# A second group entered plainly, audits pinned in order, and transposes ahead of scores, in a fused gated-attention and MLP kernel

## The chip, the cores and the metric

One core of one Trainium2 chip. The time is the device time of one execution in microseconds, the median of three runs. PE is the tensor engine, DVE VectorE, ACT ScalarE, POOL GpSimd, SP the engine that issues all transfers here.

## The reference

Recurrent gated linear attention (4 sequences, 8 heads, 768 tokens, head size 48), whose output, 3072 tokens by 384, goes through an MLP with SiLU:

```python
for t in range(S):
    state = alpha[:, :, t, :, None] * state + einsum('bhd,bhe->bhde', k[:, :, t], v[:, :, t])
    y[:, :, t] = einsum('bhd,bhde->bhe', q[:, :, t], state)
x = y.transpose(0, 2, 1, 3).reshape(3072, 384)
h = x @ w_in                       # 384 x 2048
out = (h / (1 + exp(-h))) @ w_out  # 2048 x 384
```

The kernel takes float32 q, k, v, alpha and 64-bit weights, which it turns into float32 itself.

## The kernel before

**Chunks.** The tokens are cut into 24 chunks of 128 (6 places in a sequence, 4 sequences; chunk n has place n // 4, so chunks 0 to 3 begin their sequences). A chunk n goes through four stages: `products` transposes a, k and q on PE (line 620), copies the decay out with ACT (622) and runs two scans and two products on DVE (625 to 636), which give `u`, `p`; `scores` multiplies them (647), masks the scores on DVE (651) and transposes k back (655); `values` makes the output (680), which ACT puts into `xt`; `states` updates the recurrent state (693, 699). Each step of the main loop emits scores(n-1), products(n), values(n-1), states(n-1) in this order, with a slot of other work behind each stage.

**The MLP.** Four chunks make a group, six groups in all. `enter` multiplies a group by w_in with a fast block scheme of 20 block products (`PRODUCTS`) instead of 24; it needs sums of blocks of x (`sums_x`, 11 on DVE) and of w_in (`sums_w`, 23 on DVE, some in place), and DVE puts the products together (770) before SiLU (767). `enter_plain` is the ordinary product (737), with SiLU straight from PSUM (740). `leave` is the output by w_out: plain for the first half of group 0 (884), a fast scheme of 7 steps (857) otherwise, which needs `differences` of blocks of w_out (540 to 542, 897) and sums of its own input (`side_by_side`, 845; 862). A matmul of float32 has two records in the profile. Before, group 0 is entered plainly and groups 1 to 5 by the scheme.

**Weights and audit.** SP loads 12 blocks of w_in and 16 of w_out as bit pairs (461); ACT and DVE turn each into float32 (564, 567 to 569). Later `audit` reads alpha (9 transfers), w_in (12) and w_out (16) once more, 37 transfers into one buffer, and DVE reduces each to its extremes (602): 65 reduces. A flag made of them selects at the end whether a general version has to run; it doesn't here.

**Order.** Calls are emitted in the order of the main loop; `fill` runs as many `pieces` (generators of `enter`, `leave` and the rest) in a slot as a due count allows. A scheduler then orders each engine's queue by its own estimates, except that instructions handed to `keep_in_program_order` keep the order in which they were emitted. Each engine runs its queue strictly in order. PSUM's eight banks are three for the attention (`ps_a`), three for w_in (`ps_m`) and two for the output (`ps_o`).

Of the kernel before, what the change touches and what calls it, by code (L numbers as in the profile page):

```python
# [355 lines left out]
def quotients(  # L356
# [19 lines left out]
    nc = tc.nc  # L376
# [37 lines left out]

    def ps_attn(n=C):
        return ps_a.tile([128, 512], F32, name="ps_a").rearrange("p (j c) -> p j c", c=n)

# [56 lines left out]
    ident = consts.tile([128, 128], F32, name="ident")  # L474
    make_identity(nc, ident)

# [44 lines left out]
    def combine(to, sa, a, sb, b):  # L521
        if sa == sb == 1:
            dve.tensor_tensor(to, a, b, ALU.add)
        elif sa == 1:
            dve.tensor_tensor(to, a, b, ALU.subtract)
        elif sb == 1:
            dve.tensor_tensor(to, b, a, ALU.subtract)
        else:
            dve.scalar_tensor_tensor(to, a, -1.0, b, ALU.mult, ALU.subtract)

    def sums_w(upto):
        while sums_done[0] < min(upto, len(SUMS_W)):
            to, sa, a, sb, b = SUMS_W[sums_done[0]]
            combine(block_w(to), sa, block_w(a), sb, block_w(b))
            sums_done[0] += 1

    sums_done = [0]

    def differences(i):
        dve.tensor_tensor(t1[:, i], b12[:, i], b11[:, i], ALU.subtract)  # L540
        dve.tensor_tensor(t2[:, i], b22[:, i], t1[:, i], ALU.subtract)
        dve.tensor_tensor(t4[:, i], b21[:, i], t2[:, i], ALU.subtract)
# [33 lines left out]
    def audit():  # L576
# [13 lines left out]
        for src, n, kind in todo:  # L590
# [4 lines left out]
            else:  # L595
                nc.sync.dma_start(t[:, 0:n, :].rearrange("p n w -> p (n w)"), src.bitcast(I32))
                x = t[:, 0:n, 1]
            i = at[kind]
            at[kind] += 1
            for which, op in ((0, ALU.max), (1, ALU.min)):  # L600
                if kind == 1 or which == 0:
                    dve.tensor_reduce(seen[kind][which][:, i : i + 1], x, axis=AX, op=op,  # L602
                                      apply_absolute_value=True)
            yield
# [7 lines left out]
    def products(n):  # L612
# [4 lines left out]
        for name in ("a", "k", "q"):  # L617
            ps[name] = ps_attn()
# [108 lines left out]
    def enter_plain(grp, h):  # L727

        if h == 0:
            for pair in range(NQ // 2):  # L730
                g_tiles(grp, pair)
        xt = xts[2 * grp + h]
        for f in range(0, NFT, 2):
# [6 lines left out]
            act.activation(gts[grp, h, q // 2][:, i : i + 2, q % 2, :], ps, AF.Silu)  # L740
# [106 lines left out]
    def out_bank(i, n):  # L847
        return outs[i].tile([128, 512], F32, name="ps_o")[:, 0:n]

    def leave(grp, h):  # L850
# [24 lines left out]
        if grp == h == 0:  # L875
# [3 lines left out]
            for j in range(HF // 2):  # L879
# [16 lines left out]
            for i in range(0, HF, 2):  # L896
                dve.tensor_tensor(b12[:, i : i + 2], b22[:, i : i + 2], b12[:, i : i + 2], ALU.subtract)
# [6 lines left out]
        def done():  # L904
            if grp == 0:
                sums_w(12 + 2 * next(steps) + 2)
# [53 lines left out]
    def both(grp):  # L960
        last = GB * grp + GB
        pieces.append((sums_x(grp), last))
        for h in range(2):
            x, y = leave(grp - 1, h), enter(grp, h)
            for _ in range(7):
                pieces.extend(((x, last), (y, last)))
# [149 lines left out]
```

## Time and profile before

| | us |
|---|---|
| median of 3 runs | 618.42 (618.08 to 619.08) |
| profiled execution, time | 622.89 |
| profiled execution, span | 621.1 |
| PE busy | 585.3 |
| DVE busy | 435.0 |
| ACT busy | 184.7 |
| POOL busy | 5.2 |

The span is the time from the first to the last instruction in the profile; the time has what lies around it as well. The busy times overlap, and an engine that is idle while another sets the pace costs nothing. An x at the end of a row is a number of instructions; in brackets stands how long an engine was idle and what ended it.

### The profile page before, as it was taken

What the parts mean: (1) busy time and instruction counts of PE and PEld (TensorE: products, weight loads), DVE (VectorE), ACT (ScalarE), POOL (GpSimd) and SP (SyncE); (2) the same over time, 40 slices, a digit from 0 to 9 for tenths busy, and PEclk for the clock granted to TensorE, in tenths of its full rate; (3) what the DMA queues carried; (4) which work ended last, traced back from release to release, by engine and by line L of the source; (5) the groups of instructions that cost most, each with busy time, mean ns of one, the idle gap of its engine ahead of it and who ended that gap; (6) DMA issues with size and microseconds to landing.
All of it is one profiled execution on the core that took longest, in us unless ns stands there. A gap on an engine that the chain in (4) does not pass through costs nothing.

```text
span 621.1 us, 10850 instructions
## 1 busy us (share of the span) xinstructions
PE 585.3 (94%) x4450; PEld 521.4 (84%) x4450; DVE 435.0 (70%) x802; ACT 184.7 (30%) x311; POOL 5.2 (1%) x22
## 2 busy tenths in 40 slices
PE   4889989998999979999999999999999999999996
PEld 3668876697777869989978999999999999999996
DVE  3897999868978798677689577479377365444531
ACT  1335441010335434134233224224233233242200
POOL 3000000000000000000000000000000000000000
PEclk9789999997999989999998999999999999999999
DMA  9986964165664524445353233033010000000000
GB/s 208 222 173 199 249 145 86 33 152 155 171 154 85 141 59 92 137 105 115 103 133 72 71 58 52 20 55 55 20 34 1 14 14 6 20 7 13 15 20 30
DMA packets 116169, 54.25 MB, mean 87 GB/s; under 512 B 101648, under 2 KB 107792, under 8 KB 116112
## 3 DMA queue, kind: packets, MB, share of 16 engines
q1 hardware_dynamic: 116112, 53.49, 37.7%
q8 instruction: 36, 0.59, 0.4%
q14 instruction: 21, 0.17, 0.1%
HBM read 48.76 MB, written 4.72 MB: 86 GB/s over the span
## 4 chain that ended last, share of the span: by engine, by line
PE 56%; DVE 27%; DMA 12%; issue 2%; ACT 1%; POOL 1%; DVEq 0%; ACTq 0%; SPq 0%; POOLq 0%
PE ps_o L857 27%; PE ps_m L756 19%; DMA bits<-in_moe_w_out_dram 5%; DMA bits<-in_moe_w_in_dram 5%; DVE seen L602 5%; PE ps_a L680 3%; PE ps_a L620 3%; DVE g L770 3%; DVE p L634 2%; DVE u L625 2%; DMA bits<-in_alpha_dram 2%; PE ps_a L647 2%; DVE u L629 1%; DVE p L636 1%; PE ps_a L655 1%
## 5 line engine op out<-in xcount | busy, mean ns | idle before, releaser
L857 PE MATMUL ps_o<-w_out,g 128*128 128x192 f32 x704 | 126.8, 335 | 0.6 <-DVE o L871 0.6
L857 PEld LDWEIGHTS ps_o<-w_out,g 128*128 128x128 f32 x704 | 118.9, 196 | 3.8 <-issue 1.4
L857 PE MATMUL ps_o<-wt,g 128*128 128x192 f32 x528 | 91.8, 327 | 0.0
L756 PE MATMUL ps_m<-xc,w_in 128*128 128x256 f32 x360 | 88.1, 380 | 1.0 <-DVE g L770 0.9
L857 PEld LDWEIGHTS ps_o<-wt,g 128*128 128x128 f32 x528 | 86.3, 190 | 1.5 <-issue 0.8
L756 PEld LDWEIGHTS ps_m<-xc,w_in 128*128 128x128 f32 x360 | 66.9, 190 | 9.6 <-DVE g L770 1.5
L602 DVE TENSOR_REDUCE seen<-bits 128x1 f32<-128x384 int32 (+2 forms) x65 | 43.2, 689 | 36.9 <-DMA bits<-in_moe_w_out_dram 16.1
L762 ACT COPY g<-ps_m 128x512 f32<-128x512 f32 x80 | 46.8, 588 | 70.2 <-PE ps_m L756 70.2
L767 ACT ACTIVATE g<-g 128x1024 f32<-128x1024 f32 x40 | 41.2, 1054 | 74.1 <-DVE g L770 74.1
L756 PE MATMUL ps_m<-xc,wx 128*128 128x256 f32 x240 | 62.2, 381 | 0.0
L862 DVE TENSOR_TENSOR g<-g 128x512 f32<-128x512 f32 x66 | 45.1, 687 | 17.0 <-PE ps_o L857 16.9
L770 DVE TENSOR_TENSOR g<-ps_m,g 128x512 f32<-128x512 f32 x70 | 46.9, 684 | 6.9 <-PE ps_m L756 5.7
L756 PEld LDWEIGHTS ps_m<-xc,wx 128*128 128x128 f32 x240 | 43.6, 190 | 5.1 <-issue 1.0
L737 PE MATMUL ps_m<-xt,w_in 128*128 128x256 f32 x192 | 45.5, 391 | 0.5 <-DVE w_in L569 0.5
L647 PE MATMUL ps_a<-p,u 48*128 48x128 f32 x384 | 30.2, 297 | 12.5 <-DVE p L636 11.8
L647 PEld LDWEIGHTS ps_a<-p,u 48*128 48x128 f32 x384 | 25.4, 198 | 19.5 <-issue 14.0
L737 PEld LDWEIGHTS ps_m<-xt,w_in 128*128 128x128 f32 x192 | 36.4, 196 | 6.2 <-DVE w_in L569 1.0
L651 DVE TENSOR_TENSOR g<-ps_a,mask 128x512 f32<-128x512 f32 x48 | 31.6, 686 | 11.6 <-PE ps_a L647 11.2
L762 ACT COPY part<-ps_m 128x512 f32<-128x512 f32 x40 | 23.5, 587 | 52.8 <-PE ps_m L756 34.6
L625 DVE TENSOR_TENSOR_SCAN u<-al,one 128x516 f32<-128x516 f32 x24 | 29.5, 1229 | 10.9 <-ACT al L622 10.8
L770 DVE TENSOR_TENSOR g<-g,part 128x512 f32<-128x512 f32 x30 | 20.5, 683 | 17.8 <-ACT part L762 12.8
L756 PE MATMUL ps_m<-xt,w_in 128*128 128x256 f32 x120 | 31.0, 381 | 0.7 <-DVE g L770 0.7
(102 smaller groups left out, 658.4 us busy)
## 6 DMA issues: line engine op xcount, KB each, us to landing
bits<-in_moe_w_in_dram SPq DMA_DIRECT2D x24, 512.0 KB, 3.8
bits<-in_moe_w_out_dram SPq DMA_DIRECT2D x32, 384.0 KB, 3.5
an<-in_alpha_dram SPq DMA_DIRECT2D x24, 192.0 KB, 4.0
kn<-in_k_dram SPq DMA_DIRECT2D x24, 192.0 KB, 4.7
qn<-in_q_dram SPq DMA_DIRECT2D x24, 192.0 KB, 4.7
vn<-in_v_dram SPq DMA_DIRECT2D x24, 192.0 KB, 3.7
bits<-in_alpha_dram SPq DMA_DIRECT2D x9, 512.0 KB, 3.9
out_dram<-o SPq DMA_DIRECT2D x48, 96.0 KB, 1.6
```

The source lines that it names most:

```text
L602: dve.tensor_reduce(seen[kind][which][:, i : i + 1], x, axis=AX, op=op, apply_absolute_value=True)
L620: pe.transpose(ps[name][:, j, :], c[name][:, 2 * j : 2 * j + 2, :], ident)
L625: dve.tensor_tensor_scan(u[:, end - 1 :: -1], sg[:, end:0:-1], one[:, end:0:-1], 0.0, ALU.mult, ALU.add)
L647: pe.matmul(ps[u][:, j, :], lhsT=c["kp"][r, j, :], rhs=c["qp"][r, j, :], start=True, stop=True)
L651: dve.tensor_tensor(g[:, u], ps[u], mask[:, None, :].to_broadcast([128, NP, C]), ALU.mult)
L737: pe.matmul(ps[:, e, :], lhsT=w_in[:, t, (f + e) * 128 : (f + e + 1) * 128], rhs=xt[:, t, :], start=(t == 0), stop=(t == NKT - 1))
L756: pe.matmul(ps[:, e], lhsT=block_w(w)[:, 2 * pair + e], rhs=block_x(grp, x), start=(first and e == 0), stop=(e == 1), skip_group_check=True)
L762: act.copy(to, ps)
L767: act.activation(x, x, AF.Silu)
L770: dve.tensor_tensor(to, a, b, op)
L857: pe.matmul(ps, lhsT=x, rhs=w[:, i], start=(first and i == 0), stop=(i == HF - 1), skip_group_check=True)
L862: dve.tensor_tensor(cells(grp, h, pair, *to), cells(grp, h, pair, *x), cells(grp, h, pair, *y), ALU.subtract)
```

## The change

1. Group 1 is entered plainly as group 0 is. `enter_plain` now takes half of a group's w_in columns at a time (`pair`); `leave(0, 1)` stands beside group 1's second half instead of ahead of group 1; the differences of w_out go into group 1's first pieces, and the sums of w_in are made by halves, in `leave(0, 1)` and `leave(1, 0)`. `sums_x(1)` and `enter(1, ...)` no longer exist.
2. An audit's reduces are emitted one call behind its transfer and keep the order of emission; audits begin with group 2's pieces.
3. In the first four steps products(n) is emitted ahead of scores(n-1), and the transposes of k and q of the first four chunks go to the two output banks.
4. A SiLU of one column at the start loads ACT's table; the identity is made earlier.
5. `fill` counts matmuls instead of pieces, and the two empty steps behind chunk 3 are gone.

```diff
+    def out_bank(i, n):
+        return outs[i].tile([128, 512], F32, name="ps_o")[:, 0:n]
...
+    table = fix.tile([128, 1], F32, name="table")
+    dve.memset(table, 0.0)
+    act.activation(table, table, AF.Silu)
+    ident = consts.tile([128, 128], F32, name="ident")
+    make_identity(nc, ident)
...
+    def sums_w(pair, upto):
+
+        r = slice(2 * pair, 2 * pair + 2)
+        while sums_done[pair] < min(upto, len(SUMS_W)):
+            to, sa, a, sb, b = SUMS_W[sums_done[pair]]
+            tc.keep_in_program_order(
+                combine(block_w(to)[:, r], sa, block_w(a)[:, r], sb, block_w(b)[:, r]))
+            sums_done[pair] += 1
+
+    sums_done = [0] * (NQ // 2)
+
+    def differences(i):
+
+        if i < HF // 2:
+            i = slice(2 * i, 2 * i + 2)
+            tc.keep_in_program_order(
+                dve.tensor_tensor(t1[:, i], b12[:, i], b11[:, i], ALU.subtract))
+            dve.tensor_tensor(t2[:, i], b22[:, i], t1[:, i], ALU.subtract)
+            dve.tensor_tensor(t4[:, i], b21[:, i], t2[:, i], ALU.subtract)
         else:
+            i -= HF // 2
+            if i % 2 == 0:
+                side_by_side(0, 1, i // 2)
+            i = slice(2 * i, 2 * i + 2)
+            dve.tensor_tensor(b12[:, i], b22[:, i], b12[:, i], ALU.subtract)
...
             else:
                 nc.sync.dma_start(t[:, 0:n, :].rearrange("p n w -> p (n w)"), src.bitcast(I32))
                 x = t[:, 0:n, 1]
+            yield
             i = at[kind]
             at[kind] += 1
             for which, op in ((0, ALU.max), (1, ALU.min)):
                 if kind == 1 or which == 0:
-                    dve.tensor_reduce(seen[kind][which][:, i : i + 1], x, axis=AX, op=op,
-                                      apply_absolute_value=True)
-            yield
+                    tc.keep_in_program_order(
+                        dve.tensor_reduce(seen[kind][which][:, i : i + 1], x, axis=AX, op=op,
+                                          apply_absolute_value=True))
...
-            ps[name] = ps_attn()
+            if n < GB and name != "a":
+
+                ps[name] = out_bank("kq".index(name), 512).rearrange("p (j c) -> p j c", c=C)
+            else:
+                ps[name] = ps_attn()
             for j in range(NP):
                 pe.transpose(ps[name][:, j, :], c[name][:, 2 * j : 2 * j + 2, :], ident)
...
-    def enter_plain(grp, h):
+    def enter_plain(grp, h, pair):
         if h == 0:
-            for pair in range(NQ // 2):
-                g_tiles(grp, pair)
+            g_tiles(grp, pair)
         xt = xts[2 * grp + h]
-        for f in range(0, NFT, 2):
+        for f in range(8 * pair, 8 * pair + 8, 2):
             ps = bank(f // 2 % 3).rearrange("p (e n) -> p e n", e=2)
             for e in range(2):
                 for t in range(NKT):
                     pe.matmul(ps[:, e, :], lhsT=w_in[:, t, (f + e) * 128 : (f + e + 1) * 128],
                               rhs=xt[:, t, :], start=(t == 0), stop=(t == NKT - 1))
             q, i = divmod(f, 4)
-            act.activation(gts[grp, h, q // 2][:, i : i + 2, q % 2, :], ps, AF.Silu)
+            act.activation(gts[grp, h, pair][:, i : i + 2, q % 2, :], ps, AF.Silu)
+            if grp == 1 and pair == 0:
+                differences(4 * h + f // 2)
+            if grp > 0 and f % 8 == 6:
+                side_by_side(grp, h, pair)
             yield
...
-                differences(slice(2 * j, 2 * j + 2))
-                if j % 2 == 1:
-                    side_by_side(0, 1, j // 2)
-                sums_w(3 * j + 3)
                 if j < HF // 2 - 1:
                     yield
...
         def done():
-            if grp == 0:
-                sums_w(12 + 2 * next(steps) + 2)
+            if 2 * grp + h in (1, 2):
+                sums_w(2 * grp + h - 1, 4 * next(steps) + 4)
...
+    def plain(grp, h, pair):
+        return (enter_plain(grp, h, pair), 12, 2 * (2 * grp + h) + 2)
+
+    def group(grp):
+        return [[(enter(grp, pair), 12, GB * grp + GB)] * 7 for pair in range(2)]
+
+    def output(grp):
+        return [[(leave(grp, h), 12, GB * grp + GB)] * 7 for h in range(2)]
+
+    def both(x, y):
+        for i in range(max(len(x), len(y))):
+            pieces.extend(x[i : i + 1] + y[i : i + 1])
     pieces = []
-    for part, n, last in ((enter_plain(0, 0), HF, 2), (enter_plain(0, 1), HF, 4),
-                          (leave(0, 0), HF // 2, 4), (leave(0, 1), 7, 4),
-                          (sums_x(1), 1, 2 * GB), (enter(1, 0), 7, 2 * GB), (enter(1, 1), 7, 2 * GB)):
-        pieces += [(part, last)] * n
-    ALONE = 15
-    START = len(pieces) - ALONE
+    for h in range(2):
+        for pair in range(2):
+            pieces += [plain(0, h, pair)] * 4
+    pieces += [(leave(0, 0), 24, GB)] * (HF // 2)
+    phases = [len(pieces)]
+    for h in range(2):
+        pieces += [plain(1, h, 0)] * 4
+    both([(leave(0, 1), 12, GB)] * 7, [plain(1, 0, 1)] * 4 + [plain(1, 1, 1)] * 4)
+    phases.append(len(pieces))
+    before = output(1)
     for grp in range(2, NG):
-        both(grp)
-    for h in range(2):
-        pieces += [(leave(NG - 1, h), NT)] * 7
+        pieces.append((sums_x(grp), 0, GB * grp + GB))
+        for x, y in zip(before, group(grp)):
+            both(x, y)
+        phases.append(len(pieces))
+        before = output(grp)
+    pieces += before[0] + before[1]
+    work_at = [0]
+    for _, n, _ in pieces:
+        work_at.append(work_at[-1] + n)
...
-    begin = [n if n < GB else n + 2 for n in range(NT)]
-    STEPS = begin[-1] + 2
-    FIRST = 4
+    STEPS = NT + 1
     SLOTS = 4
-    STEADY = (begin[2 * GB - 1] + 1) * SLOTS + 3
+    marks = [2 * SLOTS + 2] + [(GB * i + 2 * GB) * SLOTS + 2 for i in range(len(phases))]
...
-        if step < FIRST:
+        at = step * SLOTS + slot
+        if at < marks[0]:
             if step >= 1:
-                convert(0, ((step - 1) * SLOTS + slot + 1) * 6 // ((FIRST - 1) * SLOTS))
+                convert(0, (at - SLOTS) * 3 // (marks[0] - SLOTS) + 1)
             return
-        at = step * SLOTS + slot + 1
-        if at <= STEADY:
-            share = START * (at - FIRST * SLOTS) // (STEADY - FIRST * SLOTS)
-        elif at <= STEADY + GB * SLOTS:
-            share = START + ALONE * (at - STEADY) // (GB * SLOTS)
-        else:
-            share = START + ALONE + 29 * (at - STEADY - GB * SLOTS) // (GB * SLOTS)
-            if at % 2:
-                next(audits, None)
-        while done < share and pieces[done][1] <= bridged:
+        i = next(i for i, m in enumerate(marks[1:]) if at < m)
+        a, b = [work_at[n] for n in ([0] + phases)[i : i + 2]]
+        due = a + (b - a) * (at - marks[i] + 1) / (marks[i + 1] - marks[i])
+        if i >= 2 and at % 2:
+            next(audits, None)
+        while work_at[done + 1] <= due and pieces[done][2] <= bridged:
             convert(0, 3 * (done // 2) + 6)
-            convert(1, 2 * done - 8)
+            convert(1, 3 * (done - 6) // 2)
...
     for step in range(STEPS):
-        for slot, (stage, lag) in enumerate(
-                ((scores, 1), (products, 0), (values, 1), (states, 1))):
-            if step - lag in begin:
-                n = begin.index(step - lag)
+        stages = ((scores, 1), (products, 0), (values, 1), (states, 1))
+        if step < GB:
+
+            stages = stages[1::-1] + stages[2:]
+        for slot, (stage, lag) in enumerate(stages):
+            n = step - lag
+            if 0 <= n < NT:
                 stage(n)
                 if stage is values:
                     bridged = n + 1
```

How it moves instructions. PE's queue at the start; `an`, `kn`, `qn` are the inputs alpha, k and q (the numbers tell the two buffers apart), L620 and L644 the transposes, L647 and L671 the scores. Before:

```order
L620 MATMUL ps_a<-ident,an_107 128x128 x4
L620 MATMUL ps_a<-ident,kn_111 128x128 x4
L620 MATMUL ps_a<-ident,qn_109 128x128 x4
L647 MATMUL ps_a<-p,u 128x128 x8
L655 MATMUL ps_a<-ident,u 128x128 x4
L620 MATMUL ps_a<-ident,an_108 128x128 x4
L620 MATMUL ps_a<-ident,kn_112 128x128 x4
L620 MATMUL ps_a<-ident,qn_110 128x128 x4
```

PE's queue at the start, now:

```order
L644 MATMUL ps_a<-ident,an_115 128x128 x4
L644 MATMUL ps_o<-ident,kn_119 128x128 x4
L644 MATMUL ps_o<-ident,qn_117 128x128 x4
L644 MATMUL ps_a<-ident,an_116 128x128 x4
L644 MATMUL ps_o<-ident,kn_120 128x128 x4
L644 MATMUL ps_o<-ident,qn_118 128x128 x4
L671 MATMUL ps_a<-p,u 128x128 x8
L679 MATMUL ps_a<-ident,u 128x128 x4
```

Chunk 1's transposes moved ahead of chunk 0's scores, and k and q into the output banks.

PE's queue where group 1 is entered. Before, by the scheme (L756), behind all of leave(0, 1):

```order
L647 MATMUL ps_a<-p,u 128x128 x8
L655 MATMUL ps_a<-ident,u 128x128 x4
L756 MATMUL ps_m<-xc,w_in 128x256
L620 MATMUL ps_a<-ident,an_108 128x128 x4
L620 MATMUL ps_a<-ident,kn_112 128x128 x4
L620 MATMUL ps_a<-ident,qn_110 128x128 x4
L756 MATMUL ps_m<-xc,w_in 128x256 x3
L756 MATMUL ps_m<-xc,wx 128x256 x2
```

Now, plainly (L760), with leave(0, 1) (L881) in between:

```order
L671 MATMUL ps_a<-p,u 128x128 x8
L679 MATMUL ps_a<-ident,u 128x128 x4
L881 MATMUL ps_o<-w_out,g 128x192 x8
L760 MATMUL ps_m<-xt,w_in 128x256 x6
L644 MATMUL ps_a<-ident,an_115 128x128 x4
L644 MATMUL ps_a<-ident,kn_119 128x128 x4
L644 MATMUL ps_a<-ident,qn_117 128x128 x4
L881 MATMUL ps_o<-wt,g 128x192 x8
```

The products need no `xc` and no DVE combination any more, and the output steps moved in between them.

DVE's queue where the audits begin (L602, L623); L651 and L675 mask scores. Before, ahead of group 1's products:

```order
L523 TENSOR_TENSOR xc<-xt 128x256 x2
L602 TENSOR_REDUCE seen_1918<-bits 128x1
L897 TENSOR_TENSOR w_out<-w_out 128x2x192
L699 TENSOR_TENSOR st_162<-ps_a,st_162 48x4x48 x2
L602 TENSOR_REDUCE seen_1918<-bits 128x1
L897 TENSOR_TENSOR w_out<-w_out 128x2x192
L651 TENSOR_TENSOR g<-ps_a,mask 128x512 x2
L602 TENSOR_REDUCE seen_1918<-bits 128x1
```

Now, beside group 2's products (L797 puts these together, L886 is `subtract` in `leave`):

```order
L723 TENSOR_TENSOR st_165<-ps_a,st_165 48x4x48 x2
L623 TENSOR_REDUCE seen_1873<-bits 128x1
L797 TENSOR_TENSOR g<-g,part 128x512
L886 TENSOR_TENSOR g<-g 128x2x2x128 x2
L675 TENSOR_TENSOR g<-ps_a,mask 128x512 x2
L797 TENSOR_TENSOR g<-g,part 128x512
L886 TENSOR_TENSOR g<-g 128x2x2x128 x2
```

The reduces moved back by more than a group and stand between the pieces of the scheme.

More of the change, by code (lines that the diff above doesn't have):

```diff
@@ L522, in combine @@
         if sa == sb == 1:
[L523 to L527, printed above, removed]
-        else:
[L529 to L542, printed above, removed]
+            return dve.tensor_tensor(to, a, b, ALU.add)
+        if sa == 1:
+            return dve.tensor_tensor(to, a, b, ALU.subtract)
+        if sb == 1:
+            return dve.tensor_tensor(to, b, a, ALU.subtract)
+        return dve.scalar_tensor_tensor(to, a, -1.0, b, ALU.mult, ALU.subtract)
+    def sums_w(pair, upto):
[13 more added lines that the diff above has]
+            dve.tensor_tensor(t4[:, i], b21[:, i], t2[:, i], ALU.subtract)
+        else:
+            i -= HF // 2
[3 more added lines that the diff above has]
+            dve.tensor_tensor(b12[:, i], b22[:, i], b12[:, i], ALU.subtract)
     def weights(which):
@@ L845, in side_by_side @@
         dve.tensor_tensor(x, x, cells(grp, h, pair, 1, 1), ALU.add)
-    def out_bank(i, n):
-        return outs[i].tile([128, 512], F32, name="ps_o")[:, 0:n]
     def leave(grp, h):
@@ L895, in leave @@
                     store(m, c, ps[m][:, c * HO : (c + 1) * HO])
-            for i in range(0, HF, 2):
-                dve.tensor_tensor(b12[:, i : i + 2], b22[:, i : i + 2], b12[:, i : i + 2], ALU.subtract)
             yield
```

9 lines of the change are left out of this document (removed).

## Prediction

> **What bounds the kernel now.** I read the head of the page first, then the busy time of each engine in four stretches, then the chain of waits where the tensor engine (PE) never stops, then the start of the timeline. The head says that PE is nearly always occupied:
>
> ```profile
> span 621.1 us, 10850 instructions
> PE 585.3 (94%) x4450; PEld 521.4 (84%) x4450; DVE 435.0 (70%) x802; ACT 184.7 (30%) x311; POOL 5.2 (1%) x22
> ```
>
> Busy matmuls are not matmuls at full pace, so I price PE by start-to-start times where nothing holds it up. The chain of waits from 330 us on (start, us, what) gives them:
>
> ```profile
> 333.36 1.31 PE ps_a L620 x12
> 334.67 2.60 PE ps_o L857 x16
> 337.28 2.59 PE ps_m L756 x12
> 339.87 1.67 PE ps_a L680 x56
> 341.54 2.80 PE ps_o L857 x16
> 346.92 0.88 PE ps_a L693 x8
> 353.01 1.09 PE ps_a L647 x16
> 354.10 0.58 PE ps_a L655 x4
> ```
>
> So a w_in record (256 columns) costs 2.59/12 = 0.216 us, a w_out record 0.1625, and of a chunk the transposes (T) 1.31, scores with their transpose (S) 1.67, values (V) 1.87 (the matmuls behind it start 0.2 late: 2.80 against 2.60) and states (St) 0.88. An L884 piece of 16 records goes start to start in 103.50 - 98.33 = 5.17:
>
> ```profile
> 98.33 5.33 PE L884 MATMUL ps_o<-w_out,g 128*128 128x384 f32 x16
> 103.50 0.60 PE L620 MATMUL ps_a<-ident,an 128*128 128x128 f32 x4
> ```
>
> The stretches are cut where group 0's plain matmuls run freely (51.8), at the end of L884 (123.1) and where output begins beside group 2's w_in work (227.0):
>
> ```profile
> 0.00:51.80 51.80, 37.66 (x324) 29.77 (x325) 36.27 (x65) 16.13 (x26) 5.16 (x22) 0.90 0.99 193
> 51.80:123.10 71.30, 68.19 (x426) 52.38 (x425) 68.51 (x135) 21.59 (x41) 0.00 (x0) 1.00 0.56 141
> 123.10:227.00 103.90, 93.62 (x869) 81.59 (x869) 83.86 (x144) 32.44 (x55) 0.00 (x0) 0.97 0.58 141
> 227.00:621.10 394.10, 385.83 (x2836) 357.65 (x2834) 246.41 (x460) 114.55 (x190) 0.00 (x0) 0.99 0.22 50
> ```
>
> At full pace their work is: first, 4 chunks of 4.96 (V is 1.1 in a sequence's first chunk, which has no state part) and 324 - 4 x 72 = 36 plain records, 27.6; second, 156 plain records 33.7, L884 20.8, T4 to T6, S4, S5, V4, V5, St4, St5 12.8, together 67.3; third, one leave 112 x 0.1625 = 18.2, enter(1) 160 x 0.216 = 34.6, S6 to S12, T7 to T12, V6 to V11, St6 to St11 36.1, together 88.9; fourth, four enters 138, ten leaves 182, the other chunk work 60, together 380.2. All in all 564.0. Lost are therefore 24.2 + 4.0 + 15.0 + 13.9 = 57.1 us, and 5.5 of the last 13.9 lie behind the last matmul. The change can only win from these losses; PE's work it raises.
>
> In the third stretch DVE causes the loss. Line 602 is the audit's reduce. DVE takes its instructions in order, so when a reduce waits for its own transfer, all of DVE's work behind it waits too: 36.9 us in all, and it is in this stretch that PE waits for DVE:
>
> ```profile
> L602 DVE TENSOR_REDUCE seen<-bits 128x1 f32<-128x384 int32 (+2 forms) x65 | 43.2, 689 | 36.9 <-DMA bits<-in_moe_w_out_dram 16.1 <-DMA bits<-in_moe_w_in_dram 13.1 <-DMA bits<-in_alpha_dram 7.7
> 136.89 2.78 PE L857 MATMUL ps_o<-wt,g 128*128 128x192 f32 x16
> 141.91 2.08 PE L647 MATMUL ps_a<-p,u 48*128 48x128 f32 x16 [2.24 <-DVE p L636]
> 145.75 4.21 PE L857 MATMUL ps_o<-w_out,g 128*128 128x192 f32 x16
> ```
>
> After the wait of 2.24 us the same scores take 2.08 instead of 1.09 and the same 16 records 4.2 instead of 2.77: a wait is paid twice, since the granted clock falls to half.
>
> **The change part by part.**
>
> *Group 1 plainly.* 192 records in place of 160: 32 x 0.216 = +6.9 us on PE, all on the path. In return sums_x(1) and enter(1)'s DVE combinations are gone from the third stretch, and leave(0,1) goes there from before. PE's third stretch is then plain(1) 41.5, leave(0,1) 18.2, four chunks 22.9. For DVE I estimate four chunks at 6.6 (two scans, four products, the state's pieces about 1.4), 16 differences at 0.5, leave(0,1) with about ten operations at 0.6, side by side 5 x 0.6, half of the w_in sums 23 x 0.42: some 53 us beside 82 of PE. Before, DVE was busy 83.86 of 103.9 there, audits among it.
>
> ```profile
> L625 DVE TENSOR_TENSOR_SCAN u<-al,one 128x516 f32<-128x516 f32 x24 | 29.5, 1229 | 10.9 <-ACT al L622 10.8
> L651 DVE TENSOR_TENSOR g<-ps_a,mask 128x512 f32<-128x512 f32 x48 | 31.6, 686 | 11.6 <-PE ps_a L647 11.2
> ```
>
>  I expect 3 us lost instead of 15.0; ends 0 and 9 (half the drop kept by other waits).
>
> *Sums by pair.* 46 instructions of 256 columns for 23 of 512, 46 x 0.418 - 23 x 0.682 = +3.5 us of DVE, off the path: half stands beside leave(0,1), half beside leave(1,0), where DVE has a quarter of the time free.
>
> ```profile
> L523 DVE TENSOR_TENSOR xc<-xt 128x256 f32<-128x256 f32 x15 | 6.1, 418 | 0.1
> L523 DVE TENSOR_TENSOR w_in<-wx,w_in 128x512 f32<-128x512 f32 x4 | 2.6, 682 | 0.0
> ```
>
> *Audit in order.* The reduces come a slot or more behind their transfers and begin only with group 2, so all 43.2 us of DVE go to the fourth stretch, where it is busy 246 of 394 (some 20 of the 43 were there before). SP's audit transfer still waits for the reduce that frees the one buffer, and the next chunk's v load and the output stores stand behind it. By DVE's new order the two audits of a chunk come some 2 to 4 us apart, a transfer lands 3.8 us after its issue, so I expect DVE to wait a microsecond or two at some of them. That such a wait reaches PE the trace denies: between 280 and 320 DVE waited up to 2.24 us for audit transfers, and PE was full.
>
> ```profile
> 280.00:300.00 20.00, 20.00 (x163) 18.52 (x163) 14.31 (x26) 7.00 (x13) 0.00 (x0) 1.00 0.55 121
> 300.00:320.00 20.00, 19.95 (x171) 17.87 (x169) 14.97 (x31) 3.84 (x6) 0.00 (x0) 1.00 0.50 123
> 320.00:340.00 20.00, 17.85 (x111) 16.09 (x113) 19.04 (x40) 8.18 (x14) 0.00 (x0) 0.91 0.40 84
> bits<-in_moe_w_in_dram SPq DMA_DIRECT2D x24, 512.0 KB, 3.8
> 299.75 1.01 DVE L602 TENSOR_REDUCE seen<-bits 128x1 f32<-128x384 int32 x2 [2.24 <-DMA bits<-in_moe_w_out_dram]
> ```
>
> The loss at 320 to 340 is sums_x crowding DVE (19.04 of 20) as a group begins; it may come again at three group starts instead of two. I keep 13 lost in the fourth stretch, ends 10 and 20.
>
> *Table at once, transposes ahead.* The first decay copy waits 1.28 us for ScalarE's table; the second load, at 38.75, goes too, hidden.
>
> ```profile
> 5.38 1.28 ACT L622 ACT_TABLE_LOAD   x1 [5.38 <-PE ps_a L620]
> 6.67 0.59 ACT L622 COPY al<-ps_a 128x512 f32<-128x512 f32 x1
> 12.03 2.08 PE L647 MATMUL ps_a<-p,u 48*128 48x128 f32 x16 [4.37 <-DVE p L636]
> 21.29 1.16 PE L647 MATMUL ps_a<-p,u 48*128 48x128 f32 x16 [1.47 <-DVE p L636]
> 31.44 1.16 PE L647 MATMUL ps_a<-p,u 48*128 48x128 f32 x16
> 41.17 1.16 PE L647 MATMUL ps_a<-p,u 48*128 48x128 f32 x16 [1.00 <-DVE p L636]
> 14.73 1.09 SPq L436 DMA_DIRECT2D qn<-in_q_dram  x1
> 12.00:18.00 6.00, 5.91 (x64) 4.89 (x64) 2.60 (x4) 1.75 (x3) 0.00 (x0) 1.00 1.39 212
> 57.88 0.69 DVE L569 CUSTOM_DVE_ANT_0 w_in<-w_in,up 128x1024 uint16<-128x1024 uint16 x1
> 59.77 0.69 DVE L569 CUSTOM_DVE_ANT_0 w_in<-w_in,up 128x1024 uint16<-128x1024 uint16 x1
> ```
>
> The Trainium skill, page "ScalarE: Activation LUTs", section "What ACT_TABLE_LOAD costs", adds a drain of about 1.38 us to a load of 1.28 when the set is switched. Here the copy starts 0.01 us behind the load, so the measured 1.28 stands; by the page's 2.66 the sum would be 1.4 us lower at most.
>
> I walk the new order with these durations. Chunk 0's scan starts 1.3 earlier, but DVE now has chunk 1's scan ahead of p0, and PE has chunk 1's q transposes ahead of scores 0: those come at about 12.7, no gain. Chunk 1's p is ready near 15, not 21.1. Its scores, however, stand behind chunk 2's transposes in PE's order, and the transfers are the bound there (DMA share 1.39): q of chunk 2, issued at 14.73, lands near 19.9 (an estimate, five behind its issue), so scores 1 come at 20.5. p2 is ready at 26, but eight matmuls that need the third converted w_in block (28.7) stand ahead: scores 2 at 33, against 31.44. p3 is ready at 35.5, against 41.0. From there DVE converts without a pause (59.77 - 57.88 = 1.89 us a block): the twelfth block is done at 52.5, against 59.77 + 0.69 = 60.5. PE follows with 20 records: half of group 0 is entered at 56.8. By then 39.9 us of full-pace work is done (96 records, T0 to T4, S0 to S3, V0 to V2, St0 to St2), so 16.9 are lost instead of 24.2. Ends: 13 (table and transposes both pay in full) and 24 (nothing gained). I take 17, the walk. Behind it DVE has lost some 20 us of differences and sums, and PE does not wait in my walk up to L884: 2 lost instead of 4.0, ends 0 and 5.
>
> *Out banks for k and q.* Only chunks 0 to 3 use them; the first output product comes after, so nothing is held up. The ident and DVE memset moves cost nothing: PE's first transpose waits for a's transfer until 4.2 either way.
>
> **Sum.** 564.0 + 6.9 = 570.9 of work and 17 + 2 + 3 + 13 = 35 lost give a span of 605.9, 15.2 less than 621.1. The profiled execution took 622.89, the median of the runs is 618.42; I subtract from the latter: 603.
>
> **Rivals.**
> 1. *The start does not gain* (603 + 7 = 610): transfers are at 1.39 of their share, and chunk loads now go ahead of the weight blocks in SP's queue, so conversions wait for them. For it: three blocks land some 8 us later than before. Against: DVE has the next chunks to do meanwhile.
> 2. *PE never waits before group 2*, and the group starts are calm: 13 + 0 + 0 + 10 lost, 12 less than mine: 591; half of it 597.
> 3. *Slower: audits stall PE.* Pinned in DVE's order over the whole second half, the transfers make DVE wait for the same 36.9 us in all, and there every DVE wait has PE's bank drains right behind it. If PE feels it all, 603 + 37 = 640. It decides from 15.2/36.9 = 41% felt on. For it: the second half has no other slack than DVE's. Against it the two full rows from 280 to 320.
> 4. *A cold clock through the start*: PE works in short bursts between transfers until 35 us, at half clock, and the eight matmuls ahead of scores 2 take 7 instead of 3.5. DVE then waits some 2 to 3 us more: 606. For it, the clock of 0.57 between 24 and 30:
>
> ```profile
> 24.00:30.00 6.00, 5.78 (x52) 4.74 (x53) 5.47 (x9) 2.27 (x5) 0.00 (x0) 0.57 1.13 259
> ```
>
> The Trainium skill, "TensorE: Matmul & The Clock Gate", section "Part 1: The HAM clock gate (the "warmup" mystery)", has the clock halved after an idle window of about 3.4 us. The trace agrees in kind but is stricter: a gap of 2.24 us was enough at 141.91.
>
> **How the numbers follow.** Forecast 0.45 (its own range 599 to 607), rival 1 0.17, rival 2 0.16, rival 4 0.12, rival 3 0.07, and 0.03 that the parts cancel within 0.2% (1.2 us, about what this measurement tells from nothing). Faster 0.90, same 0.03, slower 0.07. From 594 to 612 all but about 0.2 are held: rival 3, the cancelling, and half of rival 2.
>
> **What would show it.** One table load, near 1 us; chunk 1's scores near 20.5; the last w_in conversion near 53; L884 (now L908) over near 124 with V7 behind it; leave(1,0) starting near 210 and no "seen" before about 200; full PE rows from there on but for the group starts. Wrong would be: conversions ending at 60; PE waits for DVE g or p behind L623 rows; plain(1) waiting for its Silu.

## The result and the profile after

The changed kernel takes 601.23 us (600.96 to 601.28, four runs) against 618.75 for the kernel before in the same set: a ratio of 0.9716, 95% interval 0.9699 to 0.9733, 17.5 us faster. A second set on another chip gave 601.21 against 620.85, 0.9676 (0.9655 to 0.9698). 603.0 was forecast, within 594 to 612.

The head of the page after the change (the profiled execution took 600.96 us), and the busy time of each engine in the four stretches of the prediction, cut at the same places of the program: half of group 0 entered, the last product of L908 done with chunk 7's values behind it, leave(1,0) begins.

```profile
span 599.2 us, 10853 instructions
PE 584.1 (97%) x4482; PEld 521.1 (87%) x4482; DVE 420.8 (70%) x787; ACT 171.1 (29%) x295; POOL 5.2 (1%) x22
0.00:59.94 59.94, 51.20 (x356) 39.63 (x356) 47.06 (x85) 20.04 (x34) 5.16 (x22) 1.00 1.01 214
59.94:125.34 65.40, 65.40 (x578) 50.53 (x577) 51.23 (x100) 19.91 (x40) 0.00 (x0) 1.00 0.59 136
125.34:207.99 82.65, 82.65 (x693) 74.15 (x689) 49.06 (x98) 17.01 (x32) 0.00 (x0) 1.00 0.26 47
207.99:599.20 391.21, 384.81 (x2866) 356.78 (x2862) 273.42 (x507) 114.14 (x190) 0.00 (x0) 1.00 0.29 73
```

In the second and third stretch PE's busy time equals the length of the stretch, and the granted clock is 1.00 throughout. With the prediction's unit prices the work in the four is 39.9, 65.5, 82.6 and 382.5 us, so the lost time is 20.0, 0, 0 and 8.7: 28.7 in place of the 57.1 of before and of the 35 forecast.

The start, in rows of the timeline (start, duration, engine, line, operation, idle time ahead of it): the first scan, the scores of chunks 0 to 2, the last conversion of w_in, and the matmuls with which half of group 0 is entered.

```profile
6.02 1.23 DVE L649 TENSOR_TENSOR_SCAN u<-al,one 128x516 f32<-128x516 f32 x1 [4.64 <-ACT al L646]
12.54 2.08 PE L671 MATMUL ps_a<-p,u 48*128 48x128 f32 x16
21.89 1.16 PE L671 MATMUL ps_a<-p,u 48*128 48x128 f32 x16
34.08 0.71 PE L671 MATMUL ps_a<-p,u 48*128 48x128 f32 x8
55.12 0.69 DVE L588 CUSTOM_DVE_ANT_0 w_in<-w_in,up 128x1024 uint16<-128x1024 uint16 x1
55.49 4.53 PE L760 MATMUL ps_m<-xt,w_in 128*128 128x256 f32 x20
```

Scores 0 come at 12.54 (forecast 12.7), scores 1 at 21.89 (20.5), scores 2 at 34.08 (33), the conversions end at 55.81 (52.5), group 0 is half entered at 59.94 (56.8).

The audits' reduces, by the view of their tile (count, shortest/median/longest ns, from when to when) and by the group of their line (busy, mean ns, idle time ahead of it):

```profile
L623 DVE TENSOR_REDUCE seen<-bits x65: 541/672/1221, 230.9 to 555.9; 128x1 f32<-128x384 int32 x32, 128x1 f32<-128x512 int32 x24, 128x1 f32<-128x1024 f32 x9
L623 DVE TENSOR_REDUCE seen<-bits 128x1 f32<-128x384 int32 (+2 forms) x65 | 42.5, 688 | 3.5 <-DMA bits<-in_moe_w_out_dram 1.8 <-DMA bits<-in_moe_w_in_dram 1.4
```

DVE waits 3.5 us for them in place of 36.9. That nearly all of this wait goes was not forecast: the prediction expected "a microsecond or two at some of them". Which part of the change moved it, and what it was worth, is what the experiments ask.

### The profile page after: what moved, and what is told of

The parts are those of the page before. It is cut to its first block, busy times and chain, and to the rows that moved or that the text cites. A ratio compares the mean times of both kernels' runs of the same rounds, so it can differ in the third digit from the quotient of the medians.

```text
span 599.2 us, 10853 instructions
## 1 busy us (share of the span) xinstructions
PE 584.1 (97%) x4482; PEld 521.1 (87%) x4482; DVE 420.8 (70%) x787; ACT 171.1 (29%) x295; POOL 5.2 (1%) x22
## 4 chain that ended last, share of the span: by engine, by line
PE 90%; DVE 6%; issue 1%; ACT 1%; POOL 1%; DVEq 0%; ACTq 0%; POOLq 0%
PE ps_o L881 32%; PE ps_m L783 22%; PE ps_m L760 12%; PE ps_a L704 6%; PE ps_a L644 4%; PE ps_a L671 4%; PE ps_o L908 3%; PE ps_a L717 3%; PE ps_a L679 2%; DVE g L797 1%; DVE u L649 1%; DVE w_in L588 1%; DVE u L653 1%; DVE w_in L587 1%; DVE p L658 0%
## 5 line engine op out<-in xcount | busy, mean ns | idle before, releaser
L881 PE MATMUL ps_o<-w_out,g 128*128 128x192 f32 x704 | 123.2, 328 | 0.8 <-ACT g L794 0.8
L881 PEld LDWEIGHTS ps_o<-w_out,g 128*128 128x128 f32 x704 | 114.8, 190 | 4.1 <-ACT g L794 1.4
L881 PE MATMUL ps_o<-wt,g 128*128 128x192 f32 x528 | 91.4, 326 | 0.0
L760 PE MATMUL ps_m<-xt,w_in 128*128 128x256 f32 x384 | 89.5, 382 | 1.2 <-DVE w_in L588 1.1
L881 PEld LDWEIGHTS ps_o<-wt,g 128*128 128x128 f32 x528 | 86.9, 190 | 1.0
L760 PEld LDWEIGHTS ps_m<-xt,w_in 128*128 128x128 f32 x384 | 70.4, 190 | 11.5 <-DVE w_in L588 2.2
L783 PE MATMUL ps_m<-xc,w_in 128*128 128x256 f32 x288 | 70.1, 379 | 0.0
L783 PEld LDWEIGHTS ps_m<-xc,w_in 128*128 128x128 f32 x288 | 53.5, 190 | 6.2
L886 DVE TENSOR_TENSOR g<-g 128x512 f32<-128x512 f32 x66 | 45.2, 688 | 15.7 <-PE ps_o L881 15.6
L789 ACT COPY g<-ps_m 128x512 f32<-128x512 f32 x64 | 37.5, 586 | 50.2 <-PE ps_m L783 50.2
L783 PE MATMUL ps_m<-xc,wx 128*128 128x256 f32 x192 | 50.1, 383 | 0.0
L623 DVE TENSOR_REDUCE seen<-bits 128x1 f32<-128x384 int32 (+2 forms) x65 | 42.5, 688 | 3.5 <-DMA bits<-in_moe_w_out_dram 1.8
L797 DVE TENSOR_TENSOR g<-ps_m,g 128x512 f32<-128x512 f32 x56 | 37.2, 682 | 6.2 <-PE ps_m L783 5.7
L675 DVE TENSOR_TENSOR g<-ps_a,mask 128x512 f32<-128x512 f32 x48 | 31.2, 684 | 12.3 <-PE ps_a L671 12.1
L783 PEld LDWEIGHTS ps_m<-xc,wx 128*128 128x128 f32 x192 | 35.0, 190 | 4.7 <-issue 1.2
L763 ACT ACTIVATE g<-ps_m 128x512 f32<-128x512 f32 x32 | 19.1, 597 | 62.8 <-PE ps_m L760 62.8
L797 DVE TENSOR_TENSOR g<-g,part 128x512 f32<-128x512 f32 x24 | 16.6, 690 | 24.5 <-ACT g L789 15.1
L671 PEld LDWEIGHTS ps_a<-p,u 48*128 48x128 f32 x384 | 24.6, 193 | 8.4 <-issue 7.9
L658 DVE TENSOR_TENSOR_SCAN p<-al,inv 128x516 f32<-128x516 f32 x24 | 29.5, 1230 | 0.6
```

The costliest lines, as they stand in the source:

```text
L671: pe.matmul(ps[u][:, j, :], lhsT=c["kp"][r, j, :], rhs=c["qp"][r, j, :], start=True, stop=True)
L675: dve.tensor_tensor(g[:, u], ps[u], mask[:, None, :].to_broadcast([128, NP, C]), ALU.mult)
L760: pe.matmul(ps[:, e, :], lhsT=w_in[:, t, (f + e) * 128 : (f + e + 1) * 128], rhs=xt[:, t, :], start=(t == 0), stop=(t == NKT - 1))
L783: pe.matmul(ps[:, e], lhsT=block_w(w)[:, 2 * pair + e], rhs=block_x(grp, x), start=(first and e == 0), stop=(e == 1), skip_group_check=True)
L789: act.copy(to, ps)
L797: dve.tensor_tensor(to, a, b, op)
```

## The experiments

All medians are of five to twelve runs. The kernel before took 620.5 to 621.1 us beside them.

### The audits' order, alone and taken away

The kernel before with only this edit (before_audit):

```diff
+            yield
             i = at[kind]
...
-                    dve.tensor_reduce(seen[kind][which][:, i : i + 1], x, axis=AX, op=op,
-                                      apply_absolute_value=True)
-            yield
+                    tc.keep_in_program_order(
+                        dve.tensor_reduce(seen[kind][which][:, i : i + 1], x, axis=AX, op=op,
+                                          apply_absolute_value=True))
```

> The kernel before with the audits in order as its only change. Theory A (the audits' order is most of the gain; letting them loose cost the changed kernel 13 us of span): 618.7 - 13 = 606, the third stretch loses 2 to 4 us in place of 15.0, the start is as before. Rival B (order and start work together, the steps with no chunk and the old start hold the rest): half of it, 612. Rival C (with the scheme for group 1, DVE has no room for audits in order either): 616 to 619.

601.55 us (600.73 to 604.05), 0.9682 (0.9660 to 0.9704): 19.3 us faster, as much as the whole change. All three expectations allowed too little. The tile's rows of before and of this kernel, and the group of its line:

```profile
L602 DVE TENSOR_REDUCE seen<-bits x65: 535/662/1221, 120.0 to 349.5; 128x1 f32<-128x384 int32 x32, 128x1 f32<-128x512 int32 x24, 128x1 f32<-128x1024 f32 x9
L604 DVE TENSOR_REDUCE seen<-bits x65: 541/672/1221, 228.9 to 557.1; 128x1 f32<-128x384 int32 x32, 128x1 f32<-128x512 int32 x24, 128x1 f32<-128x1024 f32 x9
L604 DVE TENSOR_REDUCE seen<-bits 128x1 f32<-128x384 int32 (+2 forms) x65 | 42.6, 688 | 24.7 <-DMA bits<-in_moe_w_out_dram 11.6 <-DMA bits<-in_moe_w_in_dram 8.4 <-DMA bits<-in_alpha_dram 4.7
```

Free to move, the reduces stood in DVE's order from 120.0 us on, some 110 us ahead of where they begin when they keep to the program's order. What one of them does to PE, in two rows of DVE's timeline of before: the reduce waits for its transfer until 137.01, the last step of p comes behind it at 141.08, and the scores at 141.91, which the prediction shows, wait 2.24 us for that p.

```profile
137.01 1.22 DVE L602 TENSOR_REDUCE seen<-bits 128x1 f32<-128x1024 f32 x1 [2.30 <-DMA bits<-in_alpha_dram]
141.08 0.68 DVE L636 TENSOR_TENSOR p<-ps_a,p 128x512 f32<-128x512 f32 x1
```

In the third stretch of before (123.1 to 227.0) DVE was busy for 83.9 us, some 20 of them with reduces, waited 17.2 us for audits and 2.4 us for other things: 103.5 of 103.9 us, so it had no time to spare. Cut at the same places of the program, the third and fourth stretch of before_audit are:

```profile
124.03:214.82 90.79, 89.19 (x870) 79.50 (x869) 66.51 (x118) 32.46 (x55) 0.00 (x0) 1.00 0.34 60
214.82:602.30 387.48, 381.80 (x2836) 354.42 (x2834) 265.71 (x487) 114.49 (x190) 0.00 (x0) 1.00 0.30 74
```

PE's work is the same as in before, 88.9 and 380.2 us by the prediction, so the third stretch loses 1.9 us in place of 15.0 and the fourth 7.3 in place of 13.9. DVE still waits 24.7 us for audits, all in the fourth stretch, where it is busy for only 265.7 of 387.5 us, and PE hardly notices. PE's longest waits behind 125 us, by what they waited for (total, times, longest), in before and then in this kernel (its list ends with the second row):

```profile
PE ps_a L655 <- DVE st L699: 4.6, 4, 2.2
PE ps_m L756 <- DVE g L770: 4.0, 3, 2.3
PE ps_a L647 <- DVE p L636: 3.3, 2, 2.2
```

```profile
PE ps_a L656 <- DVE st L700: 1.4, 3, 0.7
PE ps_a L648 <- DVE p L637: 0.5, 1, 0.5
```

The whole lists add up to 12.9 and 1.9 us. The rest is the clock, the last column but two: behind 125 us three stretches of before fall below full clock, two of which are shown, and the same places of this kernel do not.

```profile
140.00:160.00 20.00, 17.21 (x158) 16.43 (x160) 16.93 (x30) 1.65 (x3) 0.00 (x0) 0.83 0.58 155
220.00:240.00 20.00, 17.53 (x103) 16.05 (x103) 19.57 (x41) 7.37 (x12) 0.00 (x0) 0.91 0.28 57
```

```profile
140.00:160.00 20.00, 19.59 (x193) 17.63 (x191) 15.24 (x32) 4.00 (x7) 0.00 (x0) 1.00 0.39 73
320.00:340.00 20.00, 20.00 (x176) 18.32 (x175) 11.48 (x21) 5.56 (x11) 0.00 (x0) 1.00 0.26 71
```

(0.17 + 0.09 + 0.09) x 20 = 7.0 us of full-clock time, with 320 to 340 us at 0.91 as the prediction shows it. 11.0 of waits and 7.0 of clock make 18.0, beside 18.8 between the two spans (621.1 and 602.3). PE's busy time says much the same: for the same 4450 records it falls by 8.1 us from the 585.3 of before, so 10.7 of the 18.8 were idle time.

```profile
PE 577.2 (96%) x4450; PEld 516.0 (86%) x4450; DVE 436.3 (72%) x802; ACT 184.4 (31%) x311; POOL 5.1 (1%) x22
```

The reverse, the changed kernel with the reduces emitted as before (audit_loose):

> The changed kernel with the audits' reduces emitted as before, free to be moved ahead in DVE's order. Theory A: they move ahead of their transfers into the third stretch again, DVE waits for audit transfers about 35 us in place of 3.5, a part reaches PE at the products of chunks 6 to 12: 601.2 + 5 to 10 = 606 to 611. Rival B (the plan with plain group 1 gives DVE the room): DVE's waits come back but PE does not feel them, 601 to 603.

615.29 us (613.89 to 617.18), 14.1 more than the changed kernel: theory A, and more than it allowed. The reduces run from 112.3 to 330.7 us, DVE waits 46.7 us for them, and PE loses in two stretches that are full, or nearly, in the changed kernel. The last row is PE's longest wait between 180 and 320 us, for the mask product:

```profile
L621 DVE TENSOR_REDUCE seen<-bits 128x1 f32<-128x384 int32 (+2 forms) x65 | 43.4, 690 | 46.7 <-DMA bits<-in_moe_w_out_dram 18.5 <-DMA bits<-in_moe_w_in_dram 15.1 <-DMA bits<-in_alpha_dram 13.1
200.00:220.00 20.00, 16.51 (x142) 14.88 (x141) 15.51 (x32) 3.87 (x8) 0.00 (x0) 1.00 0.57 146
300.00:320.00 20.00, 16.50 (x140) 14.16 (x140) 17.03 (x33) 6.49 (x9) 0.00 (x0) 1.00 0.46 118
PE ps_a L643 <- DVE g L674: 4.7, 3, 3.5
```

DVE is not full there (15.51 and 17.03 of 20): it stands still with work behind it. So plain group 1, with its free DVE, does not shield PE from loose audits. Without the audits' order, the rest of the change is worth 0.9909 (0.9886 to 0.9931), 5.8 us. The pin and the reduce's place one call later were always tried together, and the audits' transfers moved with the reduces; which of these does it stays open. In the third stretch of before, though, DVE waits for no transfer but the audits'.

The changed kernel without the audits (after_no_audit):

> The changed kernel without the audits: no transfer and no reduce of them, the places for their results are filled by GpSimd at the start. Theory A (in order and behind their transfers they cost PE nothing, the span's rest from 60 us on is PE's own work): 601.2, within 1 us. Rival (42.5 us of DVE and 3.5 us of its waits hold PE back at group starts): 597 to 599.

1542.86 us, which says nothing of audits: with 1.0 in the places of the weights' extremes the flag asks for the general version, and that ran behind the output. What can be read is the main part. Its last matmuls, then the general version's first, and the last of the changed kernel:

```profile
589.86 2.76 PE L881 MATMUL ps_o<-wt,g 128*128 128x192 f32 x16
597.19 1.09 PE L186 MATMUL ps_t<-ident,an 128*128 128x128 f32 x4 [4.57 <-DMA an<-in_alpha_dram]
```

```profile
590.88 2.76 PE L881 MATMUL ps_o<-wt,g 128*128 128x192 f32 x16
```

The output ends 1.0 us earlier without audits, and counted from the end of chunk 7's values, near 125 us, the difference is 1.4 us (one execution each). So pinned audits cost about 1 us.

### Group 1 plainly

The same start and audits, but group 1 by the scheme with the old plan (scheme_for_1), and the change without its start (plain_audit, neither transposes ahead nor early table):

> The kernel before with the audits in order, the next chunk's transposes ahead and the table at once, but group 1 still by the scheme with the old spacing of its steps (two empty steps, 160 records in place of 192). Theory A (audits were about two thirds of the 15.0 us lost in the third stretch, the scheme's own DVE combinations the rest): 618.7 - 4.2 (start) - 10 = 604.5, DVE still 80 of 104 us busy there; plain group 1 is then worth some 3 us. Rival B (the scheme's combinations crowd DVE, audits matter little): 618.7 - 4.2 - 2 = 612.5, PE waits in L756-like work of group 1 for DVE. Rival C (audits were all of it, and plain group 1 only costs its 6.9 us): 618.7 - 4.2 - 15 - some of the fourth stretch = 594 to 599, a version that beats the changed kernel.

> The changed kernel without the transposes ahead and without the early table: only group 1 plainly (with the new plan and the sums by pair) and the audits in order. Against the kernel before with the audits in order alone (601.55) it prices plain group 1. Theory A (6.9 us more of matmuls, 3 to 4 us of PE's waits less): 602.5 to 605.5. Rival (plain group 1 pays for itself, the waits it removes are worth as much): 600.5 to 602.

scheme_for_1 takes 598.86 us (597.14 to 599.63), 0.9635 (0.9613 to 0.9657), rival C: 2.4 us less than the changed kernel, whose runs (600.69 to 601.39, in two sets) lie above all of its; the two intervals against the kernel before just meet. plain_audit takes 601.39 (601.26 to 603.71) against 601.55 of before_audit: the rival, the same. So plain group 1 with its plan pays for its 6.9 us of matmuls with the old start, and costs 2.4 us with the new one. What it pays with is mostly the start: by the prediction's unit prices PE loses 20.3 us in the first two stretches of plain_audit and 29.1 in those of before_audit. The last w_in conversions: with the old plan and the old start (before_audit), with the new plan and the old start (plain_audit), with the old plan and the new start (scheme_for_1):

```profile
60.18 0.69 DVE L569 CUSTOM_DVE_ANT_0 w_in<-w_in,up 128x1024 uint16<-128x1024 uint16 x1
```

```profile
53.73 0.69 DVE L585 CUSTOM_DVE_ANT_0 w_in<-w_in,up 128x1024 uint16<-128x1024 uint16 x1
```

```profile
53.35 0.69 DVE L576 CUSTOM_DVE_ANT_0 w_in<-w_in,up 128x1024 uint16<-128x1024 uint16 x1
```

The new plan alone ends the conversions 6.4 us earlier (54.42 against 60.87), table and transposes alone 6.8 us; both together, in the changed kernel, end them at 55.81. They win the same time, once. The head of the page of scheme_for_1 has the matmuls, and its stretch from 60 to 80 us what the scheme loses there:

```profile
span 595.3 us, 10835 instructions
PE 577.7 (97%) x4450; PEld 516.2 (87%) x4450; DVE 435.8 (73%) x803; ACT 184.0 (31%) x311; POOL 5.1 (1%) x22
60.00:80.00 20.00, 18.35 (x102) 15.96 (x102) 19.32 (x41) 8.55 (x16) 0.00 (x0) 0.91 0.72 202
```

PE is busy 6.4 us less than in the changed kernel (577.7 against 584.1). The clock of 0.91 and DVE at 19.32 of 20 suggested that a lighter DVE would gain more (scheme_late_sums):

```diff
-                sums_w(3 * j + 3)
+                sums_w(j + 1)
...
-                sums_w(12 + 2 * next(steps) + 2)
+                sums_w(4 + 3 * next(steps) + 3)
```

> The version with the scheme for group 1, audits in order, transposes ahead and early table (598.86), and in it the sums of w_in later: one in place of three beside each piece of leave(0,0), three in place of two beside each of leave(0,1). Eight sums of 0.68 us leave the stretch from 60 to 100 us, where DVE is busy 19.3 and 19.9 of 20 us and PE loses some 3 us, for the one from 116 to 145 us, where DVE is busy two thirds. Theory A (DVE's load is what PE loses there): 596 to 597.5. Rival (PE waits there for single chunk results, p and st, which the sums do not delay): 598.5 to 599.5.

598.54 us (596.45 to 599.07), 0.9651 (0.9627 to 0.9675): the rival, not told apart from scheme_for_1. All runs of both lie below all of the changed kernel's.

### The start: table and transposes

Each taken out of the changed kernel, the transposes alone in the kernel before, and the table without the transposes on the scheme version (scheme_table, and scheme_table_late with the later sums):

> The changed kernel without the early Silu at the start: the table is loaded ahead of the first decay copy, and once more ahead of the first Silu. Theory A (the 1.28 us lies on the chain of the first scan up to the end of group 0's entry): 601.2 + 1.3 = 602.5. Rival (transfers and conversions bound the start, the load has cover): 601.2, within 0.3.

> The changed kernel with the old order of the stages in the first four steps and k's and q's transposes in the attention's banks. Theory A: scores 1 come later, the last w_in conversion ends near 59 in place of 55.8, half of group 0 is entered near 63.5: 601.2 + 3.5 = 604.7. Rival (transposes ahead gain nothing, the 4.2 us at the start came from the table, 1.3, and from work taken from DVE): 601 to 602.

> The kernel before with the next chunk's transposes ahead of scores in the first four steps as its only change. Theory A (the start gains by itself, as the walk had it without the table): half of group 0 is entered 3 to 5 us earlier, and the audits' waits later are the same: 618.7 - 4 = 614.7. Rival (the audits move with it and take the gain back, as they are placed by the scheduler): 617 to 619.

> The kernel before with the audits in order and the table at once; the order of the start and group 1 are the old ones. The audits' order alone gave 601.55, with table and transposes ahead 598.86. Theory A (the table is most of the start's gain, as leaving it out of the changed kernel cost 2.4 us and undoing the transposes ahead cost nothing): 598 to 599.5. Rival (with the scheme, where group 0 waits longer for DVE, the transposes ahead bring the gain): 600.5 to 601.5.

> Both of the foregoing together: scheme for group 1, audits in order, table at once, old order of the start, sums of w_in later. If both hold, 596 to 597.5; if transposes ahead matter with the scheme, 1 to 2 us more than the version with them.

```
                        audits loose     audits in order, scheme   audits in order, plain
neither                 620.85 (before)  601.55 (before_audit)     601.39 (plain_audit)
transposes ahead        621.89                                     603.58 (no_table)
table                                    599.92 (scheme_table)     600.13 (no_ahead)
both                                     598.86 (scheme_for_1)     601.21 (changed)
```

scheme_table_late is at 599.81 (599.24 to 599.93). The early table is worth 1.3 to 2.4 us. The transposes ahead cost 1.0 us alone (1.0021, 1.0005 to 1.0037), 2.2 with plain group 1 and no early table, 1.1 with it, and bring 1.1 with the scheme. Differences of about 1 us are near what these runs tell apart: the runs of one kernel spread by 0.7 to 3.8 us, and the cells come from three sets on three chips. By the ratios to the kernel before of the same set, the table is worth 0.6 to 3.0 us, and the transposes cost 1.0 to 1.3, but bring 2.3 with the scheme. Several expectations missed: no_ahead came out below both of its ranges, before_ahead above both, scheme_table between them, no_table 1 us above its theory A, and scheme_table_late, which was to gain from later sums, did not. Scores 0 show the price: with transposes alone (before_ahead), with the table alone (no_ahead), with transposes and no early table (no_table):

```profile
14.65 2.08 PE L653 MATMUL ps_a<-p,u 48*128 48x128 f32 x16
```

```profile
10.81 2.08 PE L667 MATMUL ps_a<-p,u 48*128 48x128 f32 x16 [3.10 <-DVE p L656]
```

```profile
14.40 2.08 PE L668 MATMUL ps_a<-p,u 48*128 48x128 f32 x16
```

12.03 in before, 12.54 in the changed kernel: the next chunk's scan on DVE and its transposes on PE stand ahead, and scores 0 come 1.7 us later than with the table alone. Scores 1 come no earlier for it (20.65 without the transposes ahead, 21.89 with them).

## Why the prediction was right, step by step

**The size came out, its sources did not.** 15.2 us were forecast and 17.5 measured; the audits' order, which the sum priced at 0.9 us, gives all of that alone. That the total fits is luck in part: one term was far too small and two were too large.

- *Audit in order*: the mis-sized term, 0.9 us in the sum (13.9 to 13 lost in the fourth stretch), 19.3 measured. The prediction had the cause in hand: it says that a waiting reduce holds up all of DVE's work, and PE with it, in the third stretch, and that the reduces leave that stretch. It then booked the 12 us to plain group 1; before_audit, which keeps the scheme, wins 13.1 there. The sentence that failed is that the trace denies that such a wait reaches PE in the fourth stretch. There the order brings 6.6 us. The sentence rested on two full rows from 280 to 320 us, and the loss behind them was put down to `sums_x`. But in before DVE waits 7.1 us for audits between 297 and 313 us, and PE waits 2.15 us for DVE at 326.87. In before_audit, where the same `sums_x` run from 306 to 315 us and DVE waits for no audit, the same matmul waits 0.33 us, although DVE is as full:

```profile
300.00:320.00 20.00, 19.67 (x173) 18.13 (x173) 19.44 (x39) 7.41 (x12) 0.00 (x0) 1.00 0.45 102
```

  Rival 3 had the sign wrong: pinned, the reduces stand behind their transfers and cost about 1 us; loose, they cost 14 to 19.
- *Group 1 plainly*: 15.0 to 3 lost in the third stretch was forecast and 0 came, but 13.1 of the 15.0 go by the audits' order with the scheme still there. The +6.9 us of PE holds (6.4 more busy). Net with the audits in order: 0 to +2.4 us, where the sum had 5.1 of gain.
- *Table at once, transposes ahead*: 7.2 us of gain forecast. The walk's first steps hold within 1.4 us; then it is 3.3 us late at the last conversion, and lost are 20.0, not 17. The table is worth its 1.28 us or somewhat more; the transposes' sign is not settled. The walk did not ask what the new plan does by itself: with it alone the conversions already end at 54.42, so the two had next to nothing left to win. Rival 1 (the start does not gain) is wrong as it stood, since 4.2 us of the 24.2 are gone, but the transposes and the table together have only 0.2 us of that (601.39 to 601.21).
- *Second stretch*: 2 lost forecast, 0 measured. Rival 2 (PE never waits before group 2) is right for the second and third stretch and was paid for by the start.
- *Rival 4, the cold clock*, came in part. Until 18.9 us PE's records run at half pace (scores 0 take 2.08 us, scores 1 1.16), although the clock column says 1.00 there; in before they did so at first until about 15. PE works without a gap from 16.34 us up to scores 1, so what came last there was its own work, in part at half pace, and not the transfer of q that the walk took for the bound. Behind that the rival is wrong: the 0.57 between 24 and 30 us is gone, and the matmuls ahead of scores 2 run at full pace.
- *Sums by pair, ident*: nothing, as forecast; PE's list of waits names neither, and DVE is busy 49.06 of 82.65 in the third stretch. *Out banks*: that nothing is held up is not so. Transposes into them wait 1.3 us for p of chunk 0 and 0.7 us for u of chunk 2, at 11.49 and 24.33 us. What the attention's banks would have cost in their place was not tried by itself.

Added up by the chain before, before_audit, plain_audit, changed: the audits' order was forecast at 0.9 us and gave 19.3; plain group 1, with the second stretch, was forecast at 7.1 (12 + 2 - 6.9) and gave 0.2; the start was forecast at 7.2 and gave 0.2. One part under by 18 and two over by 7 each leave the 4 us by which the second set was better than the sum (the first was by 2). With the 12 us counted to the audits, they are still under by 6, and plain group 1 would have been forecast as a loss of 4.9. Without the audits' order the terms as booked would have given about 604 for a kernel that takes 615.29.

## What to carry to other kernels

A side task that waits for transfers must stand behind them in its engine's order: where a scheduler is free to move it ahead, look in the trace when its instructions run, not where the program calls them. The price of such a wait is read from the stretch where the engine that waits has no time to spare (busy time and waits together fill it), and for some time behind it, not from the stretches that happen to be full. It is paid again when the clock falls after it. Where several edits aim at one wait, ask for each what the others leave of it; here the smallest edit took it all, and the extra matmuls bought nothing beside it.

## What was not expected of the hardware

DVE's waits alone tell little: 24.7 us of them for audits (before_audit) went with 1.9 us of PE's waits behind 125 us, 36.9 us (before) with 12.9. And the clock's part is large: 7.0 us of the 18.8 between those two spans are granted clock below 1.00 in three stretches of 20 us, where the prediction counted such loss only in passing.

How long a single wait is does not settle whether the clock falls. The gap of 2.24 us at 141.91 was followed by half pace, as the prediction shows. The longest of PE's waits behind 125 us in before, 2.29 us, was not: the records behind it take their usual time, and the clock is 1.00 between 180 and 200 us. And ahead of the fall at 227 us stand only short waits, 0.93, 0.74, 1.07 and 0.66 us within 8 us, but the 16 records behind them take 4.45 us in place of 2.77:

```profile
187.78 1.13 PE L756 MATMUL ps_m<-xt,wx 128*128 128x256 f32 x4 [2.29 <-DVE g L770]
226.58 0.63 PE L655 MATMUL ps_a<-ident,u 128*128 128x128 f32 x4 [0.66 <-DVE st L699]
227.04 4.45 PE L857 MATMUL ps_o<-w_out,g 128*128 128x192 f32 x16
```

The Trainium skill, page "TensorE: Matmul & The Clock Gate", section "Part 1: The HAM clock gate (the "warmup" mystery)", has it halved after an idle window of about 3.4 us. These rows differ: the clock fell behind waits that were all shorter, and not behind each of them. So "a wait is paid twice", as the prediction has it, holds for the wait at 141.91 and not for every one.
